# Attention, MoE and SwiGLU in one kernel: the dense stages under attention done on whole float32 operands

## The chip, the cores and the metric

The kernel runs on one core of a Trainium2 chip. The metric is the device time of one execution in microseconds (us). Before the change it was 748.6 us, the median of three runs (747.32 to 749.61). The granted clock of TensorE stands beside every run; 1.00 is 2.4 GHz, 0.5 is 1.2 GHz.

## What is computed

Three layers stand one behind the other, all in float32:

```
attn_out = _attn_ref(q, k, v, s)                    # B,H,S,D = 2,8,576,64; causal, with a decay bias
x = attn_out.transpose(0, 2, 1, 3).reshape(1152, 512)
p = domain_probs / (domain_probs.sum(-1, keepdims=True) + 1e-09)
for e in range(4):                                  # mixture: w1[e] 512x1024, w2[e] 1024x512
    h = np.maximum(x @ w1[e], 0.0)
    out += p[:, e:e + 1] * (h @ w2[e])
g = out @ w_gate; val = out @ w_val                 # 512x1536 each
return ((g / (1 + np.exp(-g))) * val) @ w_out       # w_out 1536x512
```

The three weights of the last layer arrive as 8-byte floats.

## The kernel before

**Products by parts.** A dense product is not made of float32 operands. Each operand is split into a high part (a cast to the type fp32r, done by `move`) and a low part (the operand less its high part, done by `minus`). A product is then three matmuls on TensorE, high by high, high by low and low by high: L1061 to L1063 into the hidden layer, L1223 to L1225 out of it. In `Weight.make` the splitting of a loaded weight `raw` gives `wah`, `wal` (inward) or `woh`, `wol` (outward): the high part on ACT (L906 calls L306), the low part on POOL (L910 calls L319), in two pieces of 128x512 each. Hidden values are split into `hh` and `hl` (L1258 or L1260, then L1264 on DVE).

**Attention** runs over 16 pairs of heads in four groups of four. The pairs of the first two groups hold 256 query rows each and use plain float32 products for their scores (`k`, `q`); those of the last two hold 320 and use parts (`ka`, `kb`, `qa`, `qb`). For each block of rows there is a chain: scores on PE (L624, tile `sp`), the minimum on DVE (L633, `ns`), the exponential on ACT (L640), a sum and a reciprocal on DVE (L645, L646, `st`), the scaling by it (`norm`, L650, on POOL or DVE, seen as L316), transposes on PE (L670, `tp`), a copy into `p` (L306 on ACT, L308 on DVE). A pair ends with the product with v (L720, tile `po`) and the split of `po` into `xh` and `xl` for its 256 or 320 tokens (`values`, L725). `kb` gets a copy of the high part of k (`again`, L582), on POOL or ACT.

**Dense stages under attention.** As soon as the first four pairs are done, `feed` opens stages of the mixture; each covers two 128-column blocks of the hidden layer for 256 tokens (512 once the second group is done). Four stages are opened in this way. After attention the tokens that these left out follow, then stages over 512 or 640 tokens, most of them by a scheme that makes seven products in place of eight halves (`seven`, L1139; it needs sums of weights `ws` made from `sf`, and sums of x made in `sums_of_x`).

**The order.** All engines' instructions are placed ahead of time by `Plan`: every task has an engine or a choice of engines, a rank and assumed costs, and the one that can start first is written next (rank decides between equals). Dense matmuls have ranks over 10000 and a fixed order among themselves, so attention goes first. Where TensorE would stand idle for long, small matmuls `o<-ident` (L421) are put in; their result is not used. On the chip each engine then runs its queue in that fixed order.

**Narrowing.** The 8-byte weights are turned into 4-byte ones by `Narrow.make` (36 halves, each two steps on ACT, three on DVE: L816 to L829, and two transfers). `NARROW` and `CALM` set from which stage after attention, and how fast, they are given out (L1510).

## Time and profile before

| | before |
|---|---|
| time, median of three runs | 748.6 us |
| profiled execution | 747.14 us, its span 745.2 us |
| busy in the span: PE, DVE, ACT, POOL | 715.7, 621.2, 374.4, 437.3 us |
| matmul instructions in the trace | 4323 |
| granted clock, mean | 0.997 |

Matmuls are pipelined: the record of one overlaps that of the next, so a busy PE is not yet a PE that starts a matmul as often as it could. The pace of a run of matmuls is read from the distance of their starts in the timeline. Everything that is done in attention lies before about 155 us of the span; behind it stand dense stages alone.

### The profile page before, as it was taken

The numbers are of one execution on the slowest core, as the hardware profiler recorded it, in microseconds if no ns is written. First come the engines' busy times: TensorE is split into PE (matmuls) and PEld (weight loads), VectorE is DVE, ScalarE is ACT, GpSimd is POOL, SyncE is SP. The second block draws the span as 40 slices with busy tenths as digits, with TensorE's granted clock in tenths as the row PEclk, the third lists the DMA queues.
The fourth block names the chain that finished last, engine by engine and source line by source line (L and its number), as shares of the span: only waits on it lengthen the run. The fifth ranks groups of instructions, "written<-read, shape, count | busy, mean of one in ns | idle before, by whom it ended". The sixth has DMA issues, their size and how long they took to land. (4 is left out here: it accounts for less than half of the span.)

```text
span 745.2 us, 12460 instructions
## 1 busy us (share of the span) xinstructions
PE 715.7 (96%) x4323; PEld 625.8 (84%) x4323; DVE 621.2 (83%) x1266; ACT 374.4 (50%) x843; POOL 437.3 (59%) x446
## 2 busy tenths in 40 slices
PE   7898999999999999999999999999989999999997
PEld 6566767678889989898988989897788999999996
DVE  8788887659677999989998899897997888787765
ACT  5797888643234546455565554574632333232310
POOL 8555644489535455544655455778885676765321
PEclk9999999999999999999999999999999999999999
DMA  5567441021314434453354543622210101010003
GB/s 118 134 149 187 144 103 31 1 57 29 105 66 142 138 114 160 141 185 104 137 170 142 184 155 90 210 98 88 68 58 29 58 29 57 29 58 1 1 1 127
DMA packets 77230, 72.57 MB, mean 97 GB/s; under 512 B 45976, under 2 KB 56280, under 8 KB 77168
## 3 DMA queue, kind: packets, MB, share of 16 engines
q1 hardware_dynamic: 76112, 71.52, 31.4%
q8 instruction: 34, 0.56, 0.3%
q10 hardware_dynamic: 1056, 0.26, 0.2%
q14 instruction: 28, 0.23, 0.1%
HBM read 59.82 MB, written 11.80 MB: 96 GB/s over the span
## 5 line engine op out<-in xcount | busy, mean ns | idle before, releaser
L1223 PE MATMUL o<-woh,hh 128*128 128x512 f32 x396 | 156.7, 396 | 3.1 <-DVE acc_a L1307 1.2
L1225 PE MATMUL o<-woh,hl 128*128 128x512 f32 x396 | 154.8, 391 | 2.2 <-DVE hl L319 2.2
L1224 PE MATMUL o<-wol,hh 128*128 128x512 f32 x396 | 155.8, 393 | 0.0
L1180 DVE TENSOR_TENSOR cc<-cc,h 128x320 f32<-128x320 f32 (+1 forms) x288 | 127.5, 450 | 29.1 <-PE h L1163 24.2
L319 POOL TENSOR_TENSOR wal<-raw,wah 128x512 fp32r<-128x512 f32 (+1 forms) x56 | 68.6, 1238 | 65.4 <-ACT wah L306 65.3
L1161 PE MATMUL h<-xh,wsh 128*128 128x320 f32 (+1 forms) x320 | 95.0, 297 | 0.0
L1163 PE MATMUL h<-xh,wsl 128*128 128x320 f32 (+1 forms) x320 | 95.0, 297 | 0.0
L1162 PE MATMUL h<-xl,wsh 128*128 128x320 f32 (+1 forms) x320 | 94.9, 297 | 0.0
L1225 PEld LDWEIGHTS o<-woh,hl 128*128 128x128 f32 x396 | 74.4, 188 | 19.7 <-DVE hl L319 3.1
L1223 PEld LDWEIGHTS o<-woh,hh 128*128 128x128 f32 x396 | 74.5, 188 | 17.3 <-DVE acc_a L1307 2.1
L1224 PEld LDWEIGHTS o<-wol,hh 128*128 128x128 f32 x396 | 74.5, 188 | 10.8
L319 POOL TENSOR_TENSOR wol<-raw,woh 128x512 fp32r<-128x512 f32 x52 | 74.9, 1456 | 14.4 <-ACT woh L306 14.2
L1280 ACT ACTIVATE cc<-cc 128x640 f32<-128x640 f32 (+1 forms) x48 | 33.4, 695 | 93.9 <-DVE cc L1180 93.8
L1161 PE MATMUL h<-xh,wah 128*128 128x256 f32 (+1 forms) x240 | 71.3, 297 | 0.0
L1163 PE MATMUL h<-xh,wal 128*128 128x256 f32 (+1 forms) x240 | 71.1, 296 | 0.0
L1162 PE MATMUL h<-xl,wah 128*128 128x256 f32 (+1 forms) x240 | 71.0, 296 | 0.0
L319 POOL TENSOR_TENSOR hl<-cc,hh 128x512 fp32r<-128x512 f32 (+1 forms) x24 | 33.1, 1381 | 58.6 <-ACT hh L1283 47.7
L1161 PEld LDWEIGHTS h<-xh,wsh 128*128 128x128 f32 x320 | 60.4, 189 | 1.6
L1162 PEld LDWEIGHTS h<-xl,wsh 128*128 128x128 f32 x320 | 60.5, 189 | 1.4
L316 POOL TENSOR_SCALAR ns<-ns,st 128x512 f32<-128x512 f32 (+4 forms) x54 | 31.1, 577 | 51.6 <-DVE st L646 21.3
L1163 PEld LDWEIGHTS h<-xh,wsl 128*128 128x128 f32 x320 | 60.5, 189 | 0.0
L306 ACT CAST hh<-sg 128x512 fp32r<-128x512 f32 (+1 forms) x24 | 16.2, 676 | 85.7 <-DVE sg L1424 43.2
(155 smaller groups left out, 1876.7 us busy)
## 6 DMA issues: line engine op xcount, KB each, us to landing
raw<-in_moe_w SPq DMA_DIRECT2D x40, 512.0 KB
n<-hl SPq DMA_DIRECT2D x36, 256.0 KB
raw<-n SPq DMA_DIRECT2D x18, 512.0 KB
hh<-in_moe_w_gate SPq DMA_DIRECT2D x12, 512.0 KB
hh<-in_moe_w_val SPq DMA_DIRECT2D x12, 512.0 KB
hh<-in_moe_w_out SPq DMA_DIRECT2D x12, 512.0 KB
kr<-in_k SPq DMA_DIRECT2D x24, 128.0 KB
vr<-in_v SPq DMA_DIRECT2D x24, 128.0 KB
```

Source lines behind the costliest of these rows:

```text
L306: nc.scalar.copy(to, x)
L316: {"v": nc.vector, "p": nc.gpsimd}[e].tensor_scalar(to, x, by, 1.0, op0=ALU.mult, op1=ALU.mult)
L319: {"v": nc.vector, "p": nc.gpsimd}[e].tensor_tensor(to, x, f32(y), op=ALU.subtract)
L1161: nc.tensor.matmul(hp, wh, h, start=c == 0, stop=False)
L1162: nc.tensor.matmul(hp, wh, l, start=False, stop=False)
L1163: nc.tensor.matmul(hp, wl, h, start=False, stop=c == 1)
L1180: nc.vector.tensor_tensor(part(k), part(x), banks[i], op=ALU.add)
L1223: nc.tensor.matmul(op, hh[:, f, ts], wh[:, f, :], start=f == 0, stop=False)
L1224: nc.tensor.matmul(op, hh[:, f, ts], wl[:, f, :], start=False, stop=False)
L1225: nc.tensor.matmul(op, hl[:, f, ts], wh[:, f, :], start=False, stop=f == NF - 1)
L1280: nc.scalar.activation(src()[:, o], src()[:, o], AF.Relu)
```

## The change

For the stages that open under attention, operands are no longer split. Attention's result for the first two groups is copied once from `po` into a float32 tile `x32` (`keep`); its high and low parts, which later stages need, are made from that copy on POOL with a late rank (`PARTS`). A stage that opens before score chain 44 (`LASTEARLY`) takes the loaded weight `raw` and `x32` as they are: one float32 matmul where three stood, no split of its weights, and only the relu of its hidden values (`early_in`, and `outof` with `st.early`). Weights that are loaded in that time and used later are split after attention (`Weight.parts`). The copy of k's high part goes to POOL always. Narrowing begins two stages sooner (`CALM` 3 for 5, `NARROW` 23 for 24). The last 128 rows of the output are added up and stored in two halves, the second store issued from ACT.

```
-NARROW = 24
-CALM = 5
+NARROW = 23
+CALM = 3
+LASTEARLY = 44
+PARTS = 40.0
...
-                        t_ready[pi][j].append(any_of("pa", "copy", e - a, again, [hi], rank=rank + HEAD * j))
+                        t_ready[pi][j].append(any_of("p", "copy", e - a, again, [hi], rank=rank + HEAD * j))
...
+                if g < 2:
...
+                    def keep(on):
+                        move(on, x32, self.po[:, :n])
+
+                    def high32(on):
+                        move(on, xh[:, hp, dst], x32)
+
+                    def low32(on):
+                        minus(on, xl[:, hp, dst], x32, xh[:, hp, dst])
+                    tK = any_of(FOLD, "bank", n, keep, [tV], give=[(tV, ring("po", 1))], rank=i + RANK["f"])
+                    done_32[g].append(tK)
+                    tX = any_of("p", "copy", n, high32, [tK], rank=i + PARTS)
+                    done_x[g].append(any_of("p", "two", n, low32, [tX], rank=i + PARTS))
+                    return
...
+            self.early = early_units.setdefault(unit, "t" not in late and newest["i"] < LASTEARLY)
+            if self.early:
+
+                self.first, self.parts_ring, self.done = dma, rg, [dma] * PIECES
+                return
+            self.parts(rank)
...
+        if "t" in late:
+
+            for x in queue[:made["n"]]:
+                if x.early and not x.met:
+                    x.parts(WRANK + queue.index(x))
...
+                if st.early:
+                    nc.tensor.matmul(op, st.hid[:, f, ts], w.whole_piece()[:, f, :], start=f == 0, stop=f == NF - 1)
+                    return
...
+                    for c in range(c0, c0 + NC // 2):
+                        nc.tensor.matmul(box["p"][:, :n], w.whole_piece()[:, c, f * P:f * P + P], whole_x(c)[:, st.t0:st.t1],
+                                         start=c == 0, stop=c == NC - 1)
...
+                parts = 2 if last and t == NT - 1 else 1
```

**The order, PE, first dense work.** Before, seven products with v (L720, tile `po`) stand ahead of the first dense matmul (L1061, tile `h`); around it the queue read:

```order
L624 MATMUL sp<-ka_110,qa_114 128x64
L624 MATMUL sp<-kb_111,qb_115 128x64
L533 MATMUL h<-ident,kr 128x128 x4
L670 MATMUL tp<-ident,ns 128x128 x3
L1061 MATMUL h<-xh,wah 128x256
L1062 MATMUL h<-xl,wah 128x256
L1063 MATMUL h<-xh,wal 128x256
```

Now four products with v stand ahead of it (`hl` is the name under which the whole x lies, `raw` the weight as loaded):

```order
L633 MATMUL sp<-k_106,q_109 128x128
L633 MATMUL sp<-k_106,q_109 128x256
L1319 MATMUL h<-hl,raw 128x256 x2
L679 MATMUL tp<-ident,ns 128x128 x3
L633 MATMUL sp<-k_104,q_107 128x128
L542 MATMUL h<-ident,qr 128x128 x2
L633 MATMUL sp<-k_104,q_107 128x256
L729 MATMUL po<-p,vr 64x256 x2
```

Dense work has moved ahead by three pairs, two float32 matmuls at a time.

**The order, PE, end of attention.** Before, around the last product with v:

```order
L1061 MATMUL h<-xh,wah 128x512
L1062 MATMUL h<-xl,wah 128x512
L1063 MATMUL h<-xh,wal 128x512
L720 MATMUL po<-p,vr 64x320 x6
L720 MATMUL po<-p,vr 64x192 x2
L720 MATMUL po<-p,vr 64x64 x2
L1223 MATMUL o<-woh,hh 128x512
L1224 MATMUL o<-wol,hh 128x512
```

Now:

```order
L1279 MATMUL o<-raw,hh 128x512
L729 MATMUL po<-p,vr 64x320 x6
L729 MATMUL po<-p,vr 64x192 x2
L729 MATMUL po<-p,vr 64x64 x2
L1279 MATMUL o<-raw,hh 128x512
L1319 MATMUL h<-hl,raw 128x512 x2
L1279 MATMUL o<-raw,hh 128x512 x2
L1319 MATMUL h<-hl,raw 128x512 x6
L1279 MATMUL o<-raw,hh 128x512 x4
```

Counted over the whole queue, 114 dense matmuls by parts stood ahead of the last product with v (48 of 256 columns, 66 of 512). Now 27 float32 ones do (16 of 256, 11 of 512), and 29 of 512 columns stand behind it.

**The order, POOL, in the second half of attention.** Before, low parts of weights (`wal`, `wol`) stand between the scalings `ns`:

```order
L310 TENSOR_SCALAR kb_113<-ka_112 64x64
L319 TENSOR_TENSOR wal<-raw,wah 128x512 x2
L469 MEMSET kr 64x256
L469 MEMSET qr 64x512
L319 TENSOR_TENSOR wol<-raw,woh 128x512 x2
L310 TENSOR_SCALAR kb_111<-ka_110 64x512
L316 TENSOR_SCALAR ns<-ns,st 128x576
```

Now copies of k and parts of x stand there:

```order
L318 TENSOR_SCALAR ns<-ns,st 128x512
L312 TENSOR_SCALAR xh<-hl 128x256
L321 TENSOR_TENSOR xl<-hl,xh 128x256
L312 TENSOR_SCALAR kb_113<-ka_112 64x512
L312 TENSOR_SCALAR kb_113<-ka_112 64x64
L318 TENSOR_SCALAR ns<-ns,st 128x576
L318 TENSOR_SCALAR ns<-ns,st 128x384
```

In all, POOL loses the low parts of weights ahead of attention's end, and gains 15 copies of k (8 of 64x512, 7 of 64x64), 16 parts of x and 6 scalings, which leave DVE with 12 of its 18.

## Rows read from the trace of the kernel before

**Rows 1.** The page: span, and busy time of each engine.

```profile
span 745.2 us, 12460 instructions
PE 715.7 (96%) x4323; PEld 625.8 (84%) x4323; DVE 621.2 (83%) x1266; ACT 374.4 (50%) x843; POOL 437.3 (59%) x446
```

**Rows 2.** Busy time by stretch: start:end, length, then each engine's us, clock, DMA.

```profile
30.00:60.00 30.00, 27.48 (x190) 20.34 (x187) 25.29 (x115) 27.55 (x94) 15.85 (x28) 1.00 0.69 175
60.00:90.00 30.00, 26.10 (x192) 20.70 (x192) 26.64 (x87) 25.09 (x75) 18.38 (x25) 1.00 0.58 159
90.00:120.00 30.00, 28.02 (x195) 20.46 (x193) 25.20 (x90) 25.87 (x74) 14.22 (x24) 1.00 0.39 88
120.00:155.00 35.00, 33.40 (x209) 25.38 (x208) 18.91 (x68) 21.48 (x57) 16.95 (x22) 1.00 0.15 43
210.00:500.00 290.00, 288.44 (x1686) 259.69 (x1685) 260.74 (x427) 155.30 (x280) 161.71 (x142) 1.00 0.43 139
500.00:570.00 70.00, 63.30 (x394) 56.17 (x393) 63.22 (x106) 33.51 (x69) 58.69 (x57) 1.00 0.19 65
```

**Rows 3.** Timeline of PE: the float32 score product, the fourth pair's end, attention's end.

```profile
14.00 0.60 PE L624 MATMUL sp<-k,q 128*128 128x256 f32 x2
...
33.52 0.87 PE L720 MATMUL po<-p,vr 128*64 128x256 f32 x8
...
151.79 2.42 PE L720 MATMUL po<-p,vr 128*64 128x320 f32 x20
```

**Rows 4.** Timeline of PE: matmuls by parts of 256 and of 512 columns.

```profile
54.58 0.36 PE L1061 MATMUL h<-xh,wah 128*128 128x256 f32 x1
...
55.01 0.28 PE L1061 MATMUL h<-xh,wah 128*128 128x256 f32 x1
...
55.95 0.28 PE L1063 MATMUL h<-xh,wal 128*128 128x256 f32 x1
...
300.25 0.39 PE L1223 MATMUL o<-woh,hh 128*128 128x512 f32 x1
...
303.24 0.39 PE L1224 MATMUL o<-wol,hh 128*128 128x512 f32 x1
```

**Rows 5.** ACT, DVE and POOL in 0 to 155 us, groups by form: busy, mean ns.

```profile
L306 ACT CAST wah<-raw 128x512 fp32r<-128x512 f32 x10 | 6.0, 617 | 0.0
L306 ACT CAST woh<-raw 128x512 fp32r<-128x512 f32 x8 | 5.0, 629 | 0.4 <-PE o L1225 0.4
L736 DVE TENSOR_TENSOR xl<-po,xh 128x256 fp32r<-128x256 f32 x8 | 3.3, 418 | 0.0
L319 POOL TENSOR_TENSOR wal<-raw,wah 128x512 fp32r<-128x512 f32 x10 | 12.8, 1284 | 1.1 <-ACT wah L306 1.1
L319 POOL TENSOR_TENSOR wol<-raw,woh 128x512 fp32r<-128x512 f32 x8 | 10.4, 1310 | 1.3 <-ACT woh L306 1.1
L310 POOL TENSOR_SCALAR kb<-ka 64x512 fp32r<-64x512 f32 x8 | 4.9, 615 | 6.9 <-ACT ka L306 6.9
```

**Rows 6.** Timeline of POOL, DVE and PE: a scaling on DVE beside weight parts.

```profile
62.09 2.51 POOL L319 TENSOR_TENSOR wal<-raw,wah 128x512 fp32r<-128x512 f32 x2
62.87 2.02 DVE L316 TENSOR_SCALAR ns<-ns,st 128x512 f32<-128x512 f32 x1
65.03 0.63 PE L670 MATMUL tp<-ident,ns 128*128 128x128 f32 x4 [1.46 <-ACT woh L306]
68.93 0.48 DVE L316 TENSOR_SCALAR ns<-ns,st 128x512 f32<-128x512 f32 x1
```

**Rows 7.** Timeline of PE: a wait for a scaling on POOL; waits near the last layer's start.

```profile
119.48 0.66 PE L670 MATMUL tp<-ident,ns 128*128 128x128 f32 x4 [0.63 <-POOL ns L316]
...
520.18 0.50 PE L1225 MATMUL o<-woh,hl 128*128 128x512 f32 x1 [1.12 <-DVE hl L319]
...
547.70 0.42 PE L1161 MATMUL h<-xh,hh 128*128 128x320 f32 x1 [1.91 <-DVE cc L1180]
```

**Rows 8.** The last step of narrowing: duration, first and last start.

```profile
L829 DVE SCALAR_TENSOR_TENSOR hl<-hh,hl x36: 677/1110/1780, 226.6 to 505.1; 128x512 int32<-128x512 int32 x36
```

More of the change, by code (lines that the diff above doesn't have):

```diff
@@ L327, in attention_moe_swiglu, with whole_x @@
     done_x = {g: [] for g in range(len(groups))}
+    done_32 = {g: [] for g in range(2)}
     newest = {"i": 0}
+    def whole_x(c):
+        if "x32" not in late:
+            late["x32"] = [late["hA"].tile([P, NF, HALF], F32, name="hl", tag="hl", bufs=2) for _ in range(NC // NF)]
+        return late["x32"][c // NF][:, c % NF, :]
     def pieces():
@@ L744, in values @@
                     add(None, 0.0, None, spent_v[pi // 2], give=[(loaded[pi // 2, "v"], ring("rawv", NRV))])
+                if g < 2:
+                    x32 = whole_x(hp)[:, dst]
+                    def keep(on):
[9 more added lines that the diff above has]
+                    return
                 tX = any_of(FOLD, "bank", n, high, [tV], rank=i + RANK["f"])
@@ L853, in __init__ @@
             self.whole = False
+            self.early = self.met = False
         def load(self):
@@ L889, in make, with whole_piece, parts @@
             self.parts_ring = ring(self.tag)
+            self.dma, self.ring_raw = dma, rg
+            unit = queue.index(self) // 2
+            self.early = early_units.setdefault(unit, "t" not in late and newest["i"] < LASTEARLY)
[3 more added lines that the diff above has]
+            self.parts(rank)
+        def whole_piece(self):
+            return self.raw.rearrange("p (c n) -> p c n", n=DM if self.outward else FU)
+        def parts(self, rank):
+            self.early = False
+            self.seven = not self.outward and "t" in late
+            self.done, self.first, self.sums_done = [], None, {}
+            self.parts_ring = ring(self.tag)
+            dma, rg = self.dma, self.ring_raw
             reads = []
@@ L956, in halves @@
             return [t1, t2, t3, t4]
-    chain_w = {}
+    chain_w, early_units = {}, {}
     turns = {"h": 0, "o": 0}
@@ L1015, in __init__ @@
             self.first = None
+            self.early = False
         def tile(self):
+            if self.early:
+                if not hasattr(self, "hid"):
+                    self.hid = late["hA"].tile([P, NF, HALF], F32, name="hh", tag="hh", bufs=2)[:, :, :self.t1 - self.t0]
+                return self.hid
             if not hasattr(self, "hid"):
@@ L1231, in make @@
                     give = [(st.first, st.ring)] + ([(w.first, w.parts_ring)] if last else [])
-                x = dense_pe(3 * pe(DM), run, deps, take=[] if f else [ring("o")], give=give)
+                x = dense_pe(pe32(DM) if st.early else 3 * pe(DM), run, deps, take=[] if f else [ring("o")], give=give)
                 if f == 0:
@@ L1244, in attention_moe_swiglu, with early_in, item, run @@
     last_acc = {}
+    def early_in(w, st):
+        w.met = st.early = True
+        items = []
+        n = st.t1 - st.t0
+        for f in range(NF):
+            box = {}
+            def item(c0, f=f, box=box):
+                def run():
+                    if c0 == 0:
+                        box["p"] = bank("h")
+                    for c in range(c0, c0 + NC // 2):
+                        nc.tensor.matmul(box["p"][:, :n], w.whole_piece()[:, c, f * P:f * P + P], whole_x(c)[:, st.t0:st.t1],
+                                         start=c == 0, stop=c == NC - 1)
+                def make(last):
+                    deps = w.done + [x for g in range(2) if place[g] < st.t1 for x in done_32[g]]
+                    give = [(w.first, w.parts_ring)] if c0 and f == NF - 1 else []
+                    t = dense_pe(NC // 2 * pe32(n), run, deps, take=[] if c0 else [ring("h")], give=give)
+                    if c0 == 0:
+                        box["t"] = t
+                        return t
+                    def relu(on):
+                        if on == "a":
+                            nc.scalar.activation(st.tile()[:, f, :], box["p"][:, :n], AF.Relu)
+                        else:
+                            nc.vector.tensor_scalar(st.tile()[:, f, :], box["p"][:, :n], 0.0, None, op0=ALU.max)
+                    a = any_of(HHIGH, "bank", n, relu, [t, st.first], take=[] if st.first else [st.ring],
+                               give=[(box["t"], ring("h"))], rank=prompt())
+                    st.first = st.first or a
+                    st.lows[f, st.t0, n] = a
+                    return t
+                return make
+            items += [item(0), item(NC // 2)]
+        return items
     def moe1_in(w, st):
+        if w.early:
+            return early_in(w, st)
         if w.seven and ("T", st.t0) in late:
@@ L1465, in jobs @@
         while "h" not in late:
-            t1 = EARLY if len(done_x[1]) < NP or any(x.end is None for x in done_x[1]) else HALF
+            t1 = EARLY if len(done_32[1]) < NP or any(x.end is None for x in done_32[1]) else HALF
             part.append(t1)
@@ L1499, in stages @@
                 items = moe1_in(w_in[i], st)
+                w_out[i].met = True
                 tails = items[-1:]
@@ L1579, in attention_moe_swiglu @@
         while any(x.end is None for g in done_x for x in done_x[g]):
-            if all(x.end is not None for x in done_x[0]):
+            if len(done_32[0]) == NP and all(x.end is not None for x in done_32[0]):
                 feed()
```

23 lines of the change are left out of this document (13 added, 10 removed).

## The prediction

> **What bounds the kernel now.** I read the page first: of a span of 745.2 us PE is busy 715.7 [rows 1]. Then the busy time by stretch [rows 2]. Two regimes are to be seen. From 210 to 500 us PE is busy 288.4 of 290: there the kernel is as long as PE's matmuls, and work on the other engines is covered unless it makes PE wait. Up to 155 us, under attention, PE, DVE and ACT share the load: in 30 to 120 us PE is busy 81.6 of 90, DVE 77.1, ACT 78.5. No engine is full; each waits for the chain of another. In 120 to 155 us DVE (18.9 of 35) and ACT (21.5) fall back while PE has 33.4: there dense work fills PE. Last I read the timelines of PE for paces and single waits. Attention ends at 154.2 us (151.79 plus 2.42) [rows 3].
>
> So two quantities decide. One is how much PE work stands behind attention's end, since it runs at full pace. The other is when attention ends. A little is added by the idle PE of 500 to 570 us, 6.7 us [rows 2].
>
> **Part 1, dearer products.** A float32 matmul shows as two records. For 256 columns the two together take 0.60 us [rows 3]; a matmul by parts of 256 columns costs 0.1175 us from start to start (0.94 us over 8 steps from 55.01 to 55.95), one of 512 columns 0.23 us (2.99 us over 13 steps from 300.25) [rows 4]. The float32 pace of a long run is not in the trace, as there is none. Its upper bound is that pair's whole 0.60 us; the lower bound is the three matmuls by parts that it replaces, 0.35. If each record streams its columns twice, the matmul has four passes, 1024 columns at 2.4 GHz (the granted clock is 1.00 here): 0.43 us, and 0.86 for 512 columns. I take that: it leaves 0.17 us of latency in the 0.60, as a part's record (0.28) has over its pace (0.12) [rows 4]. The change makes 16 such matmuls of 256 columns and 16 of 512 into the hidden layer and 24 of 512 out of it, where three each stood. That is 16 x (0.43 - 0.35) = 1.3 us and 40 x (0.86 - 0.69) = 6.8 us, together **8.1 us more on PE**; the bounds are 0 and 16 x 0.25 + 40 x 0.51 = 24 us.
>
> **Part 2, what stands behind attention.** Before, 48 matmuls by parts of 256 columns and 66 of 512 stand ahead of the last product with v: 48 x 0.1175 + 66 x 0.23 = 20.8 us. Now it is 16 of 256 and 11 of 512 in float32: 16 x 0.43 + 11 x 0.86 = 16.4 us. With the 8.1 us, 8.1 + 20.8 - 16.4 = 12.5 us more stand behind attention. So **attention must end before 154.2 - 12.5 = 141.7 us, or the kernel becomes slower**.
>
> **Part 3, what attention is rid of.** ACT loses 18 casts of weights, 11.0 us [rows 5], and the copies of k that it still made; DVE loses the 8 low parts of x of the first groups, 3.3 us [rows 5], the low parts of hidden values and 6 scalings; POOL loses 18 low parts of weights, 23.2 us. POOL gains 8 copies of k at 0.615 us [rows 5] and 7 short ones, 16 parts of x (of 128x256, not in the trace in this form: between the 0.418 of such a subtraction on DVE and, scaled, half of the 1.3 us of a 128x512 one on POOL; I take 0.6, so 9.6 us), and 6 scalings. POOL's sum hardly moves, and it is the least busy (48.5 of 90 us in 30 to 120) [rows 2]. What this is worth is bounded by PE's idle time, since PE has to do the rest anyway: in 30 to 155 us it is 2.5 + 3.9 + 2.0 + 1.6 = 10.0 us [rows 2], and more by start to start, as a wait under 0.16 us hides in the record before it. I put it together from three terms.
>
> First, the scalings. At 62.87 us a scaling on DVE takes 2.02 us, though one of the same shape takes 0.48 (at 68.93). Two weight parts run on POOL from 62.09 to 64.60; the scaling ends 0.29 us later, and PE waits 1.46 us for it (the row names ACT, which had long been done) [rows 6]. I found six scalings on DVE stretched in this way beside weight parts, this being the worst. Their removal is worth between 1.5 and 9 us (six at this price); I take **3**, nearer to the one row.
>
> The Trainium skill has a rule for this (SBUF — State Buffer, section "SBUF: two separate sides"): a GpSimd instruction holds the port pair that it shares with VectorE for its whole length, and a VectorE instruction that needs it "fully blocks". The rows agree: 2.02 us instead of 0.48. The rule also speaks against the change, since copies of k and parts of x on POOL hold the port too; by it the 12 scalings left on DVE could each meet one of them.
>
> Second, dense work begins three pairs sooner, after the fourth pair (33.52 us [rows 3]) instead of at 54.58 us [rows 4]; it can fill PE's idle time of 30 to 60 us, 2.5 us. I take **2**; bounds 0 and 2.5.
>
> Third, the lighter ACT and DVE. Of PE's 10.0 us idle the first two terms use 5; of the rest and of the short hidden waits I take **6**, with bounds 0 and 9. So attention ends 11 us sooner by fewer waits, and another 20.8 - 16.4 = 4.4 us sooner by less dense work in it: at about 139 us.
>
> **Part 4, narrowing and the end.** The last narrowing step starts at 505.1 us and takes about 1.1 [rows 8], just ahead of the stretch in which DVE is busy 63.2 of 70 us and POOL 58.7 [rows 2]. There PE waits for low parts on DVE (1.12 us) and for DVE's sums (1.91) [rows 7]. Given out two stages sooner, narrowing ends sooner by about as much; Of the 6.7 us I take **2**, with bounds -1 (DVE is nearer to full while it runs) and 4. The halves of the last addition, the store on ACT, and the splits of weights that now come after attention I cost at nothing: the first two are under a microsecond, and the splits run on POOL and ACT under 29 float32 matmuls of 0.86 us, 25 us of PE; without that cover one weight's two parts would cost 2 x 1.28 = 2.6 us [rows 5].
>
> **Sum.** 745.2 + 8.1 - 11 - 2 = 740.3 us of span. The profiled execution lasted 747.14 us, 1.9 more than its span, and the median of the runs was 1.5 above it: 743.7 us.
>
> **Rivals.** *POOL becomes late (slower).* Scalings and copies of k stand in one fixed queue on POOL, and transposes on PE wait for the scalings. At 119.48 us PE waited 0.63 us for a scaling [rows 7]. With 15 more copies and 16 parts of x in that queue, one such wait for each new copy costs 15 x 0.63 = 9.5 us: 743.7 + 9.5 = 753.2 us. Against it: POOL is idle nearly half the time in this stretch. It decides from the point where attention ends after 141.7 us.
>
> *No net effect.* Attention's chains are bound by their own latency, so that lighter engines just wait longer; only the first two terms of Part 3 and narrowing remain: 745.2 + 8.1 - 5 - 2 = 746.3, so 749.7 us. For it: no engine is full in 30 to 120 us. The same end comes if POOL's new copies stretch DVE's scalings as the weights did: the 3 us of the first term are not gained, 746.7 us. The 12 scalings left, at 0.615 us each [rows 5], bound the stretching by 7.4 us of DVE. The Trainium skill's port rule (SBUF — State Buffer, "SBUF: two separate sides") is the rule by which it would come out so.
>
> *PE closes its gaps.* Attention becomes PE's own work: Part 3 gives 16 us (5 + 2 + 9, each term at or near its upper bound) and Part 4 its 4: 745.2 + 8.1 - 16 - 4 = 733.3, so 736.7 us. For it: ACT and DVE both lose over a tenth of their load there.
>
> *The change doesn't do what it says.* If the float32 stages waited for their loads or did not come forward, the order would show it; it shows them three pairs sooner, so I give this no chance of its own.
>
> **How the numbers follow.** The forecast, 743.7 us, has 0.42; closed gaps 0.15; no net effect 0.19 (0.07 of it by stretched scalings); POOL late 0.24. The range from 736 to 756 reaches from closed gaps to a change that gains nothing for its 8.1 us (756.7), and leaves out the upper bound of the float32 price. A measurement of this kernel can tell about 0.3% from no change, 2.2 us. Faster has 0.42 + 0.15 = 0.57, the same 0.19, slower 0.24.
>
> **What would show it.** In the changed kernel's timeline, float32 matmuls of 512 columns start records 0.43 us apart: if 0.35 or 0.6, Part 1 is wrong. The last product with v starts near 137 us; after 141.7 Part 3 is wrong. No scaling on DVE in 30 to 130 us takes over 1.2 us; if several do, POOL's copies took the weights' place. PE's waits for scalings on POOL show whether the first rival holds. The last step of narrowing starts before 480 us, and PE's idle time at the start of the last layer falls below 5 us, or Part 4 is wrong. The whole fails most easily in the third term: 6 us without a row of its own.

## The result: 0.96% slower, and the profile after

The changed kernel takes **754.32 us** (median of 4 runs, 753.57 to 757.16) against 748.38 us for the kernel before on the same chip: a ratio of **1.0096, 95% interval 1.0073 to 1.0118**. It is slower by about 6 us, where 4.9 less were forecast. The profiled execution took 754.01 us, of which the span is 752.1.

The page of the changed kernel, span and busy time, to lay beside [rows 1]:

```profile
span 752.1 us, 12349 instructions
PE 722.8 (96%) x4272; PEld 619.6 (82%) x4272; DVE 602.6 (80%) x1238; ACT 362.5 (48%) x811; POOL 449.4 (60%) x475
```

DVE is rid of 18.6 us and ACT of 11.9, POOL has 12.1 more; PE is busy 7.1 us longer and the span has grown by 6.9. The relief of DVE and ACT did not shorten the span.

Busy time by stretch, same columns as [rows 2]:

```profile
30.00:60.00 30.00, 27.78 (x189) 21.40 (x188) 22.22 (x109) 24.61 (x86) 19.69 (x42) 1.00 0.70 176
60.00:90.00 30.00, 29.21 (x210) 22.56 (x210) 24.84 (x95) 24.75 (x73) 16.08 (x31) 1.00 0.58 134
90.00:120.00 30.00, 28.17 (x179) 21.18 (x180) 22.38 (x84) 20.86 (x62) 11.96 (x23) 1.00 0.22 57
...
155.00:210.00 55.00, 50.94 (x205) 37.09 (x204) 32.61 (x46) 17.91 (x36) 30.50 (x28) 0.94 0.28 91
...
500.00:570.00 70.00, 67.32 (x418) 61.27 (x417) 64.50 (x111) 40.27 (x85) 64.53 (x66) 1.00 0.19 61
```

In 30 to 120 us PE is fuller than before (85.2 of 90 against 81.6), as planned. The row to stop at is 155 to 210: PE idles 4.1 of 55 us and its granted clock is 0.94. This is the stretch just behind attention, where the prediction expected 25 us of float32 matmuls to hide everything.

The last product with v, and what follows it, in the timeline of PE of the changed kernel:

```profile
139.66 2.42 PE L729 MATMUL po<-p,vr 128*64 128x320 f32 x20
...
148.47 5.39 PE L1319 MATMUL h<-hl,raw 128*128 128x512 f32 x12 [1.90 <-DMA raw<-in_moe_w]
...
158.84 3.60 PE L1279 MATMUL o<-raw,hh 128*128 128x512 f32 x8
165.53 0.72 PE L1118 MATMUL h<-xh,wah 128*128 128x512 f32 x1 [3.09 <-ACT wah L308]
166.05 0.63 PE L1119 MATMUL h<-xl,wah 128*128 128x512 f32 x1
167.64 0.80 PE L1120 MATMUL h<-xh,wal 128*128 128x512 f32 x1 [0.96 <-POOL wal L321]
168.24 0.63 PE L1118 MATMUL h<-xh,wah 128*128 128x512 f32 x1
168.66 0.63 PE L1119 MATMUL h<-xl,wah 128*128 128x512 f32 x1
```

Attention ends at 142.1 us (139.66 plus 2.42) instead of 154.2 [rows 3]. Then PE waits for the load of a weight, and, once the float32 products run out, for a weight's high part on ACT and its low part on POOL. From 168.24 on, products by parts of 512 columns start 0.42 to 0.43 us apart, where 0.23 was the pace [rows 4]. The windows around it give the reason:

```profile
165.60:172.40 6.80, 5.84 (x13) 4.17 (x14) 0.00 (x0) 1.62 (x4) 5.68 (x5) 0.50 0.25 79
172.40:180.00 7.60, 7.60 (x24) 4.35 (x24) 2.88 (x4) 1.11 (x2) 0.00 (x0) 1.00 0.28 70
```

The granted clock is 0.50 for 6.8 us (1.2 GHz of 2.4), behind a wait.

Hardly any of the 3.09 us of that wait (162.44 to 165.53) is the load. The same stretch, first the windows, then a row of ACT:

```profile
160.00:162.50 2.50, 2.44 (x6) 0.76 (x4) 2.50 (x4) 0.82 (x2) 2.50 (x4) 1.00 0.68 210
162.50:163.50 1.00, 0.00 (x0) 0.00 (x0) 0.96 (x2) 0.00 (x0) 1.00 (x2) 1.00 0.00 0
...
163.78 0.46 ACT L308 CAST xh<-tt 128x320 fp32r<-128x320 f32 x1 [1.32 <-DVE tt L1157]
```

The load of this weight is issued at 159.04 us, and from 162.5 to 163.5 no DMA moves anything: it has landed. But in ACT's fixed queue casts for the sums of x (`xh<-tt`) stand ahead of the cast of the weight, and they wait for DVE and POOL. The weight's high part is begun at 164.87. POOL in turn works on parts of the same sums until it begins the low part at 166.33.

### Work and waits of PE, one table for all kernels

To compare kernels I split each span in two. For every matmul I take the time from its start to the start of the next one, and take off the pace of its shape at full clock (by parts 0.23 us for 512 columns and 0.12 for 256, a float32 record 0.43 and 0.22, a transpose 0.11). What is left over I call waits; a stretch at half clock counts in it too. Span less waits is PE's work. The small matmuls `o<-ident`, which the plan puts in where PE would stand idle, count as work here: 59 of 0.11 us in the kernel before and in e6, 64 in the changed one and in e1, e3 and e9 to e11, 76 in e13 and e14. The paces fit to a few per cent (the undisturbed last 165 us come out at -2 us), so differences of about 1 us mean nothing, and single profiles of a kernel differ by 1 to 3 us through half-clock stretches that come at other places.

| kernel | span | attention ends | work | all waits | to 30 us | 30 us to its end | next 60 us | on to 500 | 500 to 580 |
|---|---|---|---|---|---|---|---|---|---|
| before | 745.2 | 154.2 | 702.1 | 43.1 | 12.2 | 22.1 | 1.9 | 0.3 | 8.6 |
| changed | 752.1 | 142.1 | 710.9 | 41.2 | 11.3 | 14.9 | 9.4 | 3.9 | 3.8 |
| e1, weights out of `raw` | 746.4 | 144.5 | 710.6 | 35.8 | 12.1 | 16.5 | 0.1 | 5.2 | 3.9 |
| e3, changed, narrowing as before | 752.9 | 142.7 | 710.6 | 42.3 | 12.2 | 14.6 | 8.7 | 0.2 | 8.6 |
| e6, before, sooner narrowing | 750.9 | 154.2 | 702.1 | 48.8 | 12.2 | 22.1 | 1.9 | 9.7 | 3.9 |
| e9, e1 with 12 products twice | 755.4 | 145.4 | 720.9 | 34.5 | 11.2 | 15.7 | 0.1 | 5.6 | 3.9 |
| e10, e1 with three early units | 745.2 | 146.7 | 707.9 | 37.3 | 13.3 | 17.5 | 0.2 | 4.4 | 3.9 |
| e11, e10, narrowing as before | 747.0 | 148.6 | 707.8 | 39.1 | 11.5 | 21.2 | 0.3 | -0.5 | 8.6 |
| e13, no float32, narrowing as before | 744.7 | 154.7 | 704.1 | 40.6 | 14.0 | 20.3 | 0.1 | -0.4 | 8.6 |
| e14, no float32 | 745.8 | 152.8 | 704.0 | 41.9 | 12.4 | 20.0 | 0.6 | 7.0 | 3.9 |

In each row, "its end" is attention's end and the next 60 us are counted from it; what is left to the span's end is -2 (-1 in e6). The two top rows are the result: 8.8 us more work (0.5 of it five more of the small matmuls), 7.2 us fewer waits under attention, **7.5 us more waits behind it**, and narrowing's exchange (3.6 more to 500 us, 4.8 fewer after). The sum, +8.8 - 7.2 - 0.9 + 7.5 + 3.6 - 4.8 = +7.0, is the span's 6.9.

### The profile page after: what moved, and what is told of

Read it like the earlier page. It is cut to its first block, busy times and chain, and to the rows that moved or that the text cites. A ratio compares the mean times of both kernels' runs of the same rounds, so it can differ in the third digit from the quotient of the medians.

```text
span 752.1 us, 12349 instructions
## 1 busy us (share of the span) xinstructions
PE 722.8 (96%) x4272; PEld 619.6 (82%) x4272; DVE 602.6 (80%) x1238; ACT 362.5 (48%) x811; POOL 449.4 (60%) x475
## 4 chain that ended last, share of the span: by engine, by line
PE 62%; DVE 9%; issue 4%; DMA 3%; POOL 2%; ACT 1%; SPq 0%; DVEq 0%; ACTq 0%; POOLq 0%
PE h L1218 10%; PE h L1220 10%; PE h L1219 10%; PE o L1283 9%; PE o L1284 9%; PE o L1285 9%; DVE cc L1237 2%; DVE hl L855 1%; PE h L1120 1%; PE h L1118 1%; PE h L1119 1%; DMA hh<-in_moe_w_val 1%; DVE acc_b L1407 1%; PE o L1279 1%; DMA hh<-in_moe_w_gate 1%
## 5 line engine op out<-in xcount | busy, mean ns | idle before, releaser
L1285 PE MATMUL o<-woh,hl 128*128 128x512 f32 x372 | 145.6, 391 | 4.3 <-DVE hl L321 3.3
L1283 PE MATMUL o<-woh,hh 128*128 128x512 f32 x372 | 146.8, 395 | 0.5 <-DVE acc_a L1407 0.3
L1284 PE MATMUL o<-wol,hh 128*128 128x512 f32 x372 | 146.4, 394 | 0.0
L321 POOL TENSOR_TENSOR wal<-raw,wah 128x512 fp32r<-128x512 f32 (+1 forms) x48 | 58.6, 1235 | 68.3 <-ACT wah L308 59.0
L1285 PEld LDWEIGHTS o<-woh,hl 128*128 128x128 f32 x372 | 69.9, 188 | 21.0 <-DVE hl L321 4.2
L1283 PEld LDWEIGHTS o<-woh,hh 128*128 128x128 f32 x372 | 70.0, 188 | 13.4 <-DVE acc_b L1407 2.1
L321 POOL TENSOR_TENSOR hl<-cc,hh 128x512 fp32r<-128x512 f32 (+1 forms) x29 | 43.6, 1504 | 59.0 <-ACT hh L1383 48.8
L1284 PEld LDWEIGHTS o<-wol,hh 128*128 128x128 f32 x372 | 70.0, 188 | 10.1
L321 POOL TENSOR_TENSOR wol<-raw,woh 128x512 fp32r<-128x512 f32 x44 | 65.6, 1503 | 20.1 <-ACT woh L308 20.0
L1380 ACT ACTIVATE cc<-cc 128x640 f32<-128x640 f32 (+1 forms) x48 | 33.3, 693 | 82.9 <-DVE cc L1237 82.7
L318 POOL TENSOR_SCALAR ns<-ns,st 128x384 f32<-128x384 f32 (+4 forms) x60 | 34.9, 583 | 47.3 <-DVE st L655 17.5
L1407 DVE SCALAR_TENSOR_TENSOR acc_b<-o,pr,acc_b 128x512 f32<-128x512 f32 x75 | 55.6, 744 | 5.8 <-PE o L1285 5.4
```

What stands on the lines that cost most here:

```text
L318: {"v": nc.vector, "p": nc.gpsimd}[e].tensor_scalar(to, x, by, 1.0, op0=ALU.mult, op1=ALU.mult)
L321: {"v": nc.vector, "p": nc.gpsimd}[e].tensor_tensor(to, x, f32(y), op=ALU.subtract)
L1283: nc.tensor.matmul(op, hh[:, f, ts], wh[:, f, :], start=f == 0, stop=False)
L1284: nc.tensor.matmul(op, hh[:, f, ts], wl[:, f, :], start=False, stop=False)
L1285: nc.tensor.matmul(op, hl[:, f, ts], wh[:, f, :], start=False, stop=f == NF - 1)
L1380: nc.scalar.activation(src()[:, o], src()[:, o], AF.Relu)
```

## Experiments

A ratio is always to the kernel before, run on the same chip in the same batch; 0.3% is 2.2 us.

### What makes PE wait behind attention: the raw buffers (e1, e2, e7)

**Theory A:** a weight that is used whole stays in its `raw` buffer until PE is done with it. There are three such buffers. So the next weights load late, and their parts are made late. The issue of weight loads on SP, of the kernel before and then of the changed one (start, duration of the group, count), shows it:

```profile
56.38 0.95 SPq L862 DMA_DIRECT2D raw<-in_moe_w  x2
71.14 1.61 SPq L862 DMA_DIRECT2D raw<-in_moe_w  x3
83.46 0.37 SPq L862 DMA_DIRECT2D raw<-in_moe_w  x1
98.67 0.37 SPq L862 DMA_DIRECT2D raw<-in_moe_w  x1
118.06 74.27 SPq L862 DMA_DIRECT2D raw<-in_moe_w  x7
```

```profile
56.28 0.95 SPq L889 DMA_DIRECT2D raw<-in_moe_w  x2
102.61 2.11 SPq L889 DMA_DIRECT2D raw<-in_moe_w  x2
144.88 45.85 SPq L889 DMA_DIRECT2D raw<-in_moe_w  x9
```

Before, five weights are asked for between 70 and 100 us, and the next at 118.06. In the changed kernel none is between 57 and 102, and none from 105 until 144.88, when attention is over.

**e1_free_buffers** puts the outward weights of early units into the two buffers of their high part, which stand empty then; no product is changed.

```
-            self.raw = wp.tile([P, W], F32, name="raw", tag="raw", bufs=3)
+            if self.apart:
+                self.raw = wp.tile([P, W], F32, name="woh", tag="woh", bufs=2)
+            else:
+                self.raw = wp.tile([P, W], F32, name="raw", tag="raw", bufs=3)
...
-            rg = ring("raw", 3)
+            rg = ring(self.tag) if self.apart else ring("raw", 3)
```

> The changed kernel, but early outward weights are loaded into the two buffers that hold high parts of outward weights later, so they no longer sit in the three raw buffers; the first weight that is split is then loaded and cast under attention. Theory A (the changed kernel loses its gain to three raw buffers that hold whole weights until PE has used them: loads start at 144.88 and 159.04 us, PE waits 2.1 us and then 5.0 us, and its clock falls to half for 6.8 us, some 10 us in all): those waits go, 744 to 746 us, clearly under the kernel before. Theory B (what the loads cost is only part of it; the float32 price of 8.1 us and POOL's new copies hold the rest): 751 to 754 us.

Measured: 749.34 us, ratio 1.0028 (1.0011 to 1.0045). The loads on SP now:

```profile
70.51 1.15 SPq L892 DMA_DIRECT2D raw<-in_moe_w  x2
...
103.78 0.37 SPq L892 DMA_DIRECT2D raw<-in_moe_w  x1
105.51 0.38 SPq L892 DMA_DIRECT2D woh<-in_moe_w  x1
...
117.58 0.37 SPq L892 DMA_DIRECT2D raw<-in_moe_w  x1
148.98 0.37 SPq L892 DMA_DIRECT2D woh<-in_moe_w  x1
```

Two weights more are asked for at 70.51 and one more at 117.58, ahead of attention's end. The first high part is made at 108.0 us, where the changed kernel makes it at 164.87. PE's waits behind attention, as a view lists them for the 60 us after it (in total, times, longest), are these in the changed kernel:

```profile
PE h L1118 <- ACT wah L308: 3.1, 1, 3.1
PE h L1319 <- DMA raw<-in_moe_w: 1.9, 1, 1.9
PE h L1120 <- POOL wal L321: 1.0, 1, 1.0
```

In e1 the same view has no row at all, and the clock is 1.00 throughout that stretch:

```profile
155.00:210.00 55.00, 55.00 (x245) 41.75 (x244) 39.55 (x54) 17.94 (x36) 30.38 (x27) 1.00 0.29 91
```

In the table the waits there fall from 9.4 to 0.1 us. Of the 0.96% lost, 0.68% (5 us) come back; the rest of the 9.3 us is met by 0.8 more waits up to 30 us, 1.6 more under attention and 1.3 more up to 500 us. **That the buffers cause the waits behind attention is shown**: free them, and the waits go. In e1 the load and the cast come sooner and the queues of ACT and POOL are laid anew; whether another order of these queues alone would have done it was not tried. The other half of theory A is refuted: e1 is not clearly under the kernel before, it stays 0.28% above it, clear of the noise.

**e2_two_early** frees the buffers in another way, by fewer early units.

```
-LASTEARLY = 44
+LASTEARLY = 20
```

> The changed kernel with LASTEARLY 20: only the first two stages (256 tokens) take whole operands, the two of 512 tokens go by parts again as before. Float32 price falls from 8.1 to 16 x 0.08 + 8 x 0.17 = 2.7 us; raw buffers are freed by the split. Theory A: no wait for loads behind attention, so at least 754.3 - 10 = 744, plus what the parts of two more stages cost attention (2 to 4 us): 744 to 748 us. Theory B: only the price falls, 754.3 - 5.4 = 749 us.

Measured: 755.17 us, ratio 1.0092 (1.0067 to 1.0118): a miss. The wait for the load is gone, but others stand behind attention's end, at 148.5 us (loads of the next weights still start at 103.49 only):

```profile
PE o L1283 <- DVE acc_a L1407: 2.3, 1, 2.3
PE h L1118 <- ACT wah L308: 1.1, 1, 1.1
PE h L1120 <- POOL wal L321: 0.8, 1, 0.8
```

Between 208 and 500 us the same view has another 6.4 us, for DVE and POOL above all.

**e7_two_apart** joins both edits (LASTEARLY 20 and e1's buffers).

> LASTEARLY 20 (two early stages) together with the free buffers of e1: the loads of the third and fourth unit come as early as before. Theory A, now with e2's miss: in e2 the loads of the third unit still started at 103.5 us, since the two early units sat in the raw buffers till then; with that gone no wait for a weight is left behind attention, float32 price 2.7 us: 745 to 748 us. If two stages by parts under attention are worse than four whole ones for another reason (DVE and POOL loaded again): 750 us or more, with attention's end after 147 us.

Measured: 751.8 us, ratio 1.0072 (1.0051 to 1.0093). The waits behind attention are 1.8 us. Attention ends at 159.2 us, later than in any other kernel here, but not because PE waits more: from 30 us to its end there are 21.6 us of waits, against 22.1 before. More dense work stands ahead of its end, 16 float32 matmuls of 256 columns, 8 of 512 and 51 by parts of 512, by the paces above 25.5 us against 20.8. Where e7 loses its 0.72% is not pinned down; the view of waits has 4.3 us from 219.2 to 500 us, where the kernel before has 1.4 behind its own 60 us, and the early units still have their dearer products. Fewer early units are no remedy.

### Is the half clock a loss of its own? (e5)

**e5_fill_wait** puts 32 transposes whose result is dropped into the wait ahead of the first product by parts.

```
+                    for _ in range(32 if "once" not in late and "t" in late else 0):
+                        nc.tensor.transpose(box["p"][:, :P], ident, ident)
```

> The changed kernel with 32 transposes of the identity (0.11 us each, result unused) on PE just ahead of the first product by parts behind attention, so that PE works while it waits there for the weight's parts. The wait itself stays. If the half clock of 165.6 to 172.4 us is a price of its own, caused by the idle PE: the clock stays at its full level and the span falls by about 3 us, 751 us. If the clock falls because of the float32 products ahead of it, or has no part in the loss: 754 to 755 us.

Measured: 756.87 us, ratio 1.013 (1.0089 to 1.0171). The half-clock stretch at 165 us is gone, and 1.9 (load) and 1.3 us (low part) of waits remain. But waits up to 500 us rise to 7.0 from 3.9, one of them 2.26 us just ahead of 486 us with a half clock of its own behind it (0.51 from 487.0 to 490.4), and the time doesn't fall. Keeping PE occupied over a wait for weights doesn't bring the weights sooner. What the half clock alone costs stays open; in the changed kernel's profile it is the nine steps from start to start from 168.24 to 172.08, 0.43 us each instead of 0.23, some 2 us.

### Did POOL become late? (e4, e8)

The first rival had the time nearly right (753.2 us). Its mechanism was POOL's queue under attention, above all the copies of k. PE's three largest sums of waits from 30 to 142 us, before and then changed:

```profile
PE tp L670 <- POOL ns L316: 3.2, 7, 1.0
PE tp L670 <- ACT woh L306: 1.5, 1, 1.5
PE tp L670 <- ACT p L306: 1.3, 4, 0.5
```

```profile
PE tp L679 <- POOL ns L318: 1.9, 3, 1.4
PE tp L679 <- ACT p L308: 1.1, 2, 0.6
PE sp L633 <- DVE st L642: 0.7, 2, 0.4
```

Waits for scalings on POOL have become fewer, 3 of 1.9 us in all for 7 of 3.2; one of 0.4 us for a part of x on POOL (`xh`) is new. **e4_kb_choice** gives the copies of k back to the planner's choice.

```
-    t_ready[pi][j].append(any_of("p", "copy", e - a, again, [hi], rank=rank + HEAD * j))
+    t_ready[pi][j].append(any_of("pa", "copy", e - a, again, [hi], rank=rank + HEAD * j))
```

> The changed kernel with the copies of k's high part on POOL or ACT by choice, as before. If POOL's queue is what is late (first rival of the prediction): up to 9 us faster, 745 to 750 us. If the loss lies behind attention (theory A): within 1.5 us of 754.3.

Measured: 755.69 us, ratio 1.0108 (1.0077 to 1.0139): no gain, so the copies are not the loss. **e8_kb_alone** makes that edit, the other way round, in the kernel before.

> The kernel before with the copies of k's high part on POOL always, nothing else. If POOL's queue is sensitive to them (first rival of the prediction): slower than before by 0.3 to 1%. If lighter ACT is what ends attention sooner: attention's end 1 to 3 us ahead of 154.2. If neither: within 0.2%.

Measured: 748.61 us, ratio 1.0021 (1.0004 to 1.0038): no harm that matters, and no gain. Its profile is a warning: attention ends at 146.1 us, 8.1 sooner than before, and what stands behind it takes 10.2 us longer, as dense work moved from one side of the mark to the other: 78 matmuls by parts stand ahead of its end where 114 stood, 36 of 512 columns or 8.3 us less. **The end of attention alone measures nothing.** The rival's mechanism is refuted, though its time was right; e13 below, with the copies of k and the parts of x on POOL and no float32 stages, is not slower than the kernel before either.

### Is sooner narrowing worth 2 us? (e3, e6, e12)

**e3_narrow_late** takes it out of the changed kernel; **e6_narrow_alone** puts it into the kernel before; **e12_free_calm** takes it out of e1. The edit of e3 and e12, which e6 has the other way round:

```
-NARROW = 23
-CALM = 3
+NARROW = 24
+CALM = 5
```

> The changed kernel with NARROW 24 and CALM 5, as before the change. If earlier narrowing is worth the 2 us of the prediction: 756 us; if it is worth nothing or costs: 752 to 754 us.

Measured: 756.18 us, ratio 1.0118 (1.009 to 1.0146), 0.22% or 1.6 us above the changed kernel's ratio and inside both intervals: not to be told from nothing.

> The kernel before with NARROW 23 and CALM 3 alone. If narrowing two stages sooner is worth the 2 us of the prediction, here as in the changed kernel: ratio 0.997. If it only moves PE's waits to another place: within 0.2% of before, or slower.

Measured: 753.39 us, ratio **1.0094 (1.0059 to 1.0128)**: this small edit alone makes the kernel before as slow as the whole change does. PE's waits of e6 from 200 to 260 us, where the kernel before has none:

```profile
PE o L1223 <- DVE acc_b L1307: 1.4, 2, 1.0
PE h L1161 <- ACT cc L306: 1.0, 1, 1.0
PE h L1161 <- DVE hl L1264: 1.0, 1, 1.0
PE o L1225 <- POOL hl L319: 1.0, 1, 1.0
PE h L1161 <- DVE cc L1180: 0.7, 1, 0.7
```

The last step of narrowing first starts at 201.2 us, where it was 226.6 before, and PE now waits for DVE, ACT and POOL. The 4.7 us won at the last layer (8.6 to 3.9 in the table) cost 9.4 earlier.

> e1_free_buffers (749.3) with NARROW 24 and CALM 5, the numbers of the kernel before: the second reading of the narrowing, with four early units. Theory A as for e11_three_calm: 3 to 6 us less, 743.5 to 746.5. Rival: within 1.5 us of 749.3.

Measured: 749.44 us, ratio 1.003 (1.0014 to 1.0047), the same as e1. So the price depends on the kernel that narrowing is put into: in waits from 60 us behind attention to 500 us it is 9.4 in the kernel before, 3.7 in the changed one (beside e3) and 4.9 in e10 (beside e11, below), against nearly the same saving of 4.7 or 4.8 behind 500 us.

### What do the dearer products cost? (e9, e10, e11)

**e9_twice** does 12 of e1's early products twice, at the start of a sum, where the second one starts afresh.

```
                 if st.early:
+                    if f == 0:
+                        nc.tensor.matmul(op, st.hid[:, f, ts], w.whole_piece()[:, f, :], start=True, stop=True)
                     nc.tensor.matmul(op, st.hid[:, f, ts], w.whole_piece()[:, f, :], start=f == 0, stop=f == NF - 1)
```

> The kernel with the two early outward weights in buffers of their own (e1_free_buffers, 749.3 us), and each of the 12 early outward products of a first chunk is done twice: the copy's result is dropped, since the next matmul starts the sum afresh. That adds 12 float32 matmuls of 512 columns, 2 x 0.436 us each, 10.5 us of TensorE, 3 of them before attention's end and 9 behind it (7.8 us). Theory A (the dearer products are paid in full, since TensorE is what bounds the stretch they stand in): 9 x 0.872 = 7.8 us at least, and up to 10.5, so 757 to 760. Rival (the products stand in time in which TensorE waits for weights anyway, so their price is hidden): 749 to 752, and the waits behind attention shrink.

Measured: 759.71 us, ratio 1.0156 (1.0133 to 1.018). That is 1.28% above e1, 9.6 us for 12 x 0.86 = 10.3 us of matmuls (the expectation's 0.436 us for a record took in a longer first step; later ones start 0.43 apart); in the table the work rises by 10.3 and the waits fall by 1.3. The copies stand in PE's timeline like this (L1284 the copy, L1285 the product):

```profile
157.44 1.02 PE L1285 MATMUL o<-woh,hh 128*128 128x512 f32 x2
158.30 1.02 PE L1284 MATMUL o<-woh,hh 128*128 128x512 f32 x2
159.15 1.88 PE L1285 MATMUL o<-woh,hh 128*128 128x512 f32 x4
```

**PE's price is paid nearly in full.** Hardly any of it falls into time in which PE would wait.

**e10_three_early** lets three units be early in e1 instead of four; the fourth had stood behind attention.

```
-            self.early = early_units.setdefault(unit, "t" not in late and newest["i"] < LASTEARLY)
+            self.early = early_units.setdefault(unit, "t" not in late and newest["i"] < LASTEARLY and unit < 3)
```

> e1_free_buffers with the early form for the first three units alone: the fourth unit, whose products stand behind attention, is made of parts again. That turns 16 float32 matmuls of 512 columns behind attention (0.872 us each) back into products by three parts (3 x 0.23 = 0.69). Theory A (the early form pays where it fills waits of attention and is a loss behind it): 16 x 0.18 = 2.9 us less than e1_free_buffers, so 745.5 to 747, level with the kernel before or a little under. Rival (the parts of the fourth unit then come late, since ScalarE, VectorE and GpSimd have attention's own work): a wait of 2 us or more at attention's end, and 749 or above.

Measured: 748.7 us, ratio 1.0019 (1.0001 to 1.0036). PE's work falls by 2.7 us, as 16 x 0.18 says, while waits under attention rise by 1 (and those before 30 us by 1.2). Of 2.9 us expected 0.7 arrive.

**e11_three_calm** is e10 with narrowing as before.

> e10_three_early with NARROW 24 and CALM 5, the numbers of the kernel before. Put into the kernel before, the new numbers cost 6.8 us; taken out of the changed kernel they gave nothing (756.2 against 754.3). Theory A (the narrowing from the fourth stage takes time of VectorE and GpSimd that the stages at 210 to 350 us need, wherever nothing else is late): 3 to 6 us less than e10_three_early, 741 to 744, faster than both kernels. Rival (the sooner narrowing costs only in the kernel before, whose order it upset): within 1.5 us of e10_three_early.

Measured: 747.46 us, ratio 1.001 (0.9996 to 1.0024): level with the kernel before, and not the 3 to 6 us below e10 that Theory A gave. The 21.2 us of waits under attention in its row hold a wait of 4.14 us for `p` on ACT, up to 79.39 us, and a half clock from 77.1 to 83.9; e10 waits 1.6 us for `p` there, at full clock.

### Where do the saved waits come from? (e13, e14)

**e13_no_float32_calm** keeps the rest of the change, drops the float32 stages and sets narrowing as before; the parts of x get an earlier rank.

```
-NARROW = 23
-CALM = 3
-LASTEARLY = 44
-PARTS = 40.0
+NARROW = 24
+CALM = 5
+LASTEARLY = 0
+PARTS = 6.0
```

> The changed kernel without its float32 stages (LASTEARLY 0, so that all weights have parts during attention; PARTS 6 instead of 40, so that the parts of x on GpSimd are made in time), with NARROW 24 and CALM 5 as before. What is left of the change: copies of k's high part on GpSimd alone, the parts of x of the first two groups on GpSimd from a kept float32 copy, the scalings as the planner then deals them, the last addition in two halves. TensorE's work is that of the kernel before. Theory A (the 7 to 8 us of waits that the changed kernel saves up to attention's end come from the weights' parts having left ScalarE, VectorE and GpSimd): the waits come back, and the time is 745.5 to 749, level with the kernel before. Rival (they come from what else moved to GpSimd): waits up to attention's end fall by 5 us or more without dearer products, 739 to 743, faster than both.

Measured: 745.5 us, ratio **0.9983 (0.997 to 0.9996)**, the fastest of all kernels here, though by less than 0.3%. Waits from 30 us to attention's end are 20.3 us, 1.8 below the kernel before. But that is no saving, and the 2.0 us by which its work is above the kernel before are no dearer products: both are the small matmuls put into idle time, 17 more in all. From 30 us to attention's end there are 17 of them in the kernel before, 25 in the changed one and in e1, 38 in e13. Counted as waits they make it 24.0 us before, 24.5 in e13, 17.7 in the changed kernel and 19.3 in e1. So the whole saving under attention, 6.3 us, belongs to the float32 stages, and they cost 8.8 - 0.5 = 8.3 us of PE. e12 sets the two side by side on the chip: it has float32 stages, free buffers and the old narrowing, and stands at 1.003 (1.0014 to 1.0047), e13 at 0.9983. **So the float32 stages lose 0.47%, 3.5 us, even where nothing waits behind attention for their buffers**: with these buffers some 5 us are gained under attention (24.5 to 19.3) and some 8 paid on PE. The two kernels differ in the rank of the parts of x as well, which was not tried apart, nor were the halves of the last addition; these are in e13.

**e14_no_float32** is e13 with the narrowing of the changed kernel.

> The same without float32 stages, but with NARROW 23 and CALM 3 as in the changed kernel. Put into the kernel before alone these cost 6.8 us (waits from 200 to 500 us grew from 0.3 to 9.7, those from 500 to 580 us shrank from 8.6 to 3.9); beside the float32 stages they cost nothing that can be measured. Theory A (the cost depends on the order that the other edits leave: where weights and parts of x are made in another order, the growth from 200 to 500 us is about as large as the saving after 500): within 1.5 us of e13_no_float32_calm. Rival (the cost belongs to stages by parts during attention, as in the kernel before): 4 to 7 us above e13_no_float32_calm.

Measured: 749.75 us, ratio 1.0038 (1.0024 to 1.0053), 0.55% (4.1 us) above e13; waits from 60 us behind attention to 500 us are 7.0 where e13 has none. The rival's lower bound held: where stages during attention go by parts, sooner narrowing costs 4 to 7 us (e6, e14); where they are float32, within 1.6 us either way (e3, e11, e12). Why it is so is not shown. DVE is busy 41.0 of the 45 us ahead of 200 us in e6 and 37.6 in e14, 33.3 in e1 and 24.3 in the changed kernel, so there is more room beside float32 stages; no run changed that alone.

## Why the prediction was wrong

It forecast 743.7 us and faster; it is 754.3 and slower. The sum of the span was 8.1 - 11 - 2 = -4.9, and 8.8 - 8.1 - 1.2 + 7.5 = +7.0 came. Two steps failed. The larger is a term of Part 4, the splits behind attention at nothing: 7.5 us came. The other is the size of Part 3: 8.1 us for 11. Without the first the sum would have been -0.5, no gain that could be seen; e1, which takes the waits away, is still 0.28% slower.

**Part 1, dearer products: right.** The row of 8 records at 158.84 gives (3.60 - 0.59) / 7 = 0.43 us from record to record, 0.86 for a matmul, just what was taken; the last record's own length is 0.59. The work rose by 8.8 us for 8.1 forecast, 0.5 of it the five small matmuls. e9 shows that it is paid nearly in full. The Trainium skill states that true float32 makes four passes through the array (FP8 and Floating Point Precision, "Matmul Precision"); 0.86 us over four is 0.215, near the 0.23 of one product by parts: the trace agrees.

**Part 2, the break-even: right as arithmetic, weak as a sign.** Attention ended at 142.1 us, 0.4 behind the mark of 141.7. By it the change would have been about level; the other 7 us were lost behind attention, where the mark doesn't look. e8 moved attention's end by 8.1 us without gaining anything.

**Part 3, 11 us fewer waits: 8.1 came (34.3 to 26.2 up to attention's end, 7.2 of them after 30 us, and 0.5 of them filled by small matmuls).** The first term's cause, scalings stretched beside weight parts, is gone. DVE's scalings in the changed kernel, the 18 of 0.90 us on average now 12:

```profile
L318 DVE TENSOR_SCALAR ns<-ns,st x12: 283/408/2673, 9.9 to 40.9; 128x128 f32<-128x128 f32 x7, 128x256 f32<-128x256 f32 x5
```

The last one starts at 40.9 us and none after 30 us is long, as the sign asked (0.29 us at 40.85); but this is the only one after 30 us, where nine stood before, so the sign could hardly fail. What its absence is worth was not measured apart. The long ones that are left stand ahead of 30 us, the longest of them just as long as the POOL instruction beside it:

```profile
20.70 2.60 POOL L321 TENSOR_TENSOR cums<-ncum,cums 8x1152 fp32r<-8x1152 f32 x1
...
20.71 2.67 DVE L318 TENSOR_SCALAR ns<-ns,st 128x128 f32<-128x128 f32 x1
```

Of the second term, too, the cause came: the first dense product starts at 35.27 us instead of 54.58 [rows 4]. Its size did not come where it was sought: PE's idle time of 30 to 60 us fell from 2.5 to 2.2 us, that of 60 to 90 us from 3.9 to 0.8 [rows 2]. The three terms together came out 3 short; the third, the 6 us without a row of its own, is the likeliest to have been too large, but no run parts them. The rival *No net effect* gave 5, *PE closes its gaps* 16; the truth lay between the first of these and the forecast. The Trainium skill's port rule (SBUF — State Buffer, "SBUF: two separate sides") agrees with 2.67 us beside 2.60, where 0.28 is the least of that form. Its way to no net effect, copies on POOL that stretch the scalings left on DVE, came about only in small: a scaling of 128x128 at 27.33 us took 0.66 us beside a part of x on POOL, and after 40.9 us there is none left to meet.

**Part 4: here the forecast failed.** "... the splits of weights that now come after attention I cost at nothing", since 29 float32 matmuls, 25 us of PE, would hide them. The cover was smaller than that: 21 of the 29 stand ahead of the first product by parts, 18 us, from 142 to 162 us. And the work that it should hide could not start: the loads stood behind `raw` buffers that the same matmuls kept in use, and the parts behind the loads and behind the sums of x in the queues of ACT and POOL. Four loads were issued at 144.88, 146.60, 159.04 and 162.47 us, each as PE let go of a buffer. The third is the first weight to be split; it had landed by 162.5, as the cover ended, and its high part was begun at 164.87:

```profile
164.87 1.13 ACT L308 CAST wah<-raw 128x512 fp32r<-128x512 f32 x2
```

The waits for the load, the high part and the low part are 1.9, 3.1 and 1.0 us; with the half clock behind them they make up most of the 9.4 us behind attention, where 1.9 stood before. The price that the text named for the case without cover, 2.6 us, was also too small: it counted two parts' time and neither the load nor the queue nor the clock. The rival *The change doesn't do what it says* had float32 stages that wait for their loads, and got no chance because the order showed none; one of them did wait, 1.90 us at 148.47. The order of the changed kernel showed no wait, because a buffer's release is no instruction in it; a count of `raw` buffers against early weights (three buffers, eight early weights) would have told that loads must stop.

Narrowing's 2 us came as 1.2 by the table (8.9 to 7.7 from 60 us behind attention on), not to be told from nothing in the runs. The last step starts at 480.3 us, where the sign said before 480, and PE's idle time from 500 to 570 us is 2.7 us, below 5. The first sign is missed by a hair, the second held, and both looked at the wrong side: the wait had moved ahead.

```profile
L855 DVE SCALAR_TENSOR_TENSOR hl<-hh,hl x36: 673/1075/1818, 207.8 to 480.3; 128x512 int32<-128x512 int32 x36
```

**The chances.** Slower had 0.24, all of it on a mechanism on POOL that e4 and e8 refute. That its 753.2 us lie near the 754.3 is luck: its price and the true loss happen to be alike. That the time lies inside the range is luck too: the upper end stood for a change that gains nothing for its 8.1 us, whereas here 8.1 us were gained and others lost elsewhere.

## What to carry to other kernels

- When a change keeps an input in its buffer longer, count the buffers and follow the next loads: work that is "hidden under" the matmuls that hold the buffer is not hidden, since it can't begin before they end. A load that has landed is not yet a part: its cast also has a place in a fixed queue.
- In this kernel, with PE busy 96% of the span, added work on PE cost nearly its full price (e9: 9.6 of 10.3 us), while time freed on the engines beside it paid only in part (7.2 us of waits for 30 us of DVE and ACT).
- Before calling a lower sum of waits a saving, look whether filling matmuls took their place (17 of them, 1.9 us, in e13).
- Judge by PE's work and its waits in every stretch, not by one mark such as the end of a phase: e8 moved the mark by 8 us for nothing, as 8.3 us of dense work changed sides, and narrowing swapped waits at the last layer for waits 300 us sooner.

## What the runs showed of the hardware

The half clock behind a wait I had not priced. In the changed kernel PE waited 3.09 us for a high part, started two products, waited 0.96 us, and the granted clock was 0.50 from 165.6 to 172.4 us; a product by parts of 512 columns then took 0.43 us from start to start instead of 0.23. The Trainium skill gives 426.7 ns for 512 columns at 1.2 GHz (TensorE: Matmul & The Clock Gate, Part 1, "Wait — 56ns, not 53.3ns?"); the trace agrees with 0.43. In e1, without these waits, the clock was 1.00 there. So these waits of 4 us cost some 2 us more than their length. A wait is not always followed by it: the same wait of 1.9 us for `cc` ahead of the last layer left the clock at 1.00 in the profile of the kernel before (546 to 553 us) and has 0.50 behind it in that of e12 (549.1 to 552.5 us).
